# Packed attention, gated MLP and mixture of attentions: the last score groups behind the value products, the first query product behind the packed tokens' product, the softmax chain of the next item earlier

## The chip, the cores and the metric

One of the eight cores of a Trainium2 chip runs the whole kernel in one launch. The metric is the device time of that core in microseconds (us), the median of several runs. Engines are named as the profile names them: PE (TensorE, matmuls; PEld its weight loads), DVE (VectorE), ACT (ScalarE), POOL (GpSimd) and SP, whose queue issues the DMAs.

## What is computed

Eight batch items, 576 tokens each, go through three stages.

```python
# 1: attention of 32 packed tokens p over k and v, then of q over the packed result (8 heads of 64)
p_packed = sm_attn(p, k, v)
x = sm_attn(q, p_packed, p_packed)          # then heads side by side: 576 x 512
# 2: gated MLP with a product over the tokens
h = gelu(x @ w_in); u, v = h[..., :512], h[..., 512:]
v_s = einsum('ts,bsd->btd', w_sg, layer_norm(v) * g_ln) + b_sg
x = x + (u * v_s) @ w_out
# 3: four causal attentions of head size 64, each token takes the two with the largest logits x @ w_gate
for e in range(4):
    a = softmax(causal(scale * (x @ wq[e]) @ (x @ wk[e]).T))
    out += weight_of_e * (a @ (x @ wv[e]) @ wo[e])
```

All inputs and outputs are float32.

## The kernel before

The eight items form a software pipeline. While PE works on the third stage's attention of item b-1, it also does the second stage of item b and the first stage of item b+1. Products that need float32 accuracy are made of three passes over parts `hi` and `lo` in the type fp32r (`PASSES`); the part `hi` is an ACT copy, the part `lo` a subtraction on DVE or POOL (`lo_part`, L81).

PE's instructions stand in the order in which the Python code issues them (`manual_schedule` for PE). The instructions of ACT, DVE, POOL and SP are put in order by the framework's scheduler, from dependences and priorities, before the kernel runs. Every PE result goes to one of four PSUM tiles of two banks each (`pd`, `NPS = 4`); a product can only start when an earlier user of its tile has been read out by ACT or DVE. SBUF tiles come from pools in the same way: `NB["C"] = 4` tiles hold the split attention weights `a2h`, `a2l` of both head groups Q (two each), so the tiles of item b+1 are the ones that item b's last readers give back.

One item's work, with the names that the rows use:

- First stage (`p1_steps`): `natT`, `remT` transpose k and q on PE, `kT`, `qT` are their copies; `s1` makes the packed tokens' scores (tile `s`, L349) and their softmax (`a`), `a1T` transposes it, `pp` multiplies with v (L384), `ppT` transposes the result (L401); `s2` makes q's scores over the packed tokens (tile `s` again), DVE transposes them to `bt` (L411), POOL subtracts the maximum (L417), ACT exponentiates (L418), DVE divides and transposes back to `a2f` (L425). `split_a2` makes `a2h` on ACT (L465) and `a2l` on POOL.
- Second stage: `wp_mm`, `wp_out` fold the packed tokens into the input weights (`wp`, L474, parts `wph`, `wpl`); `v_tiles` are the value products (`v`, L519) with gelu and layer norm; `u_tile` (L556); `vs_tile` is the product over tokens (L570), whose gated result is `gh`, `gl`.
- `bdw` folds the packed tokens into the third stage's weights (`bdq`, `bdv`, L474: the packed tokens' product of this change's name). `qk(b, i)` for i from 0 to 3 makes queries and keys (L599, L604), `qk_mm` the product and `qk_out` its read-out. `vlog` makes the values and gate logits (L629, L633), `gates` the gates.
- Third stage: ten work items per batch item, numbered by (128-token row block j, pair of experts pr): number 2j+pr. `S0` to `S9` are the score groups (tile `sc`): PE product, maximum `nm` on DVE, two exponentials on ACT, normalisation on DVE (`at`). S8 and S9 (`att_last`, L707 and L713) take two PSUM tiles each. `T0` to `T9` transpose the weights (`aTp`, copies `aT` on ACT), `y0` to `y4` multiply with the values, one per row block, and `o0` to `o4` are the output products with their DMAs. `y`j needs T2j and T2j+1; the loop in `yv` does the first pair, then the second.

`front` issues the value products and `u_tile`s, `back` all the rest of an item; the strings given to `go` are the third stage's work of the item before. Between the attention strings, `run` mixes the list `main` with the first-stage steps of item b+1: at each turn the list with the smaller share of its summed cost done is served. The costs (4.0, 4.8, ...) set only this order.

Of the kernel before, what the change touches and what calls it, by code (L numbers as in the profile page):

```python
# [25 lines left out]
def packed_attention_mlp_moe_kernel(  # L26
# [39 lines left out]
    def slot(tag, dt=F32, w=None, name=None):  # L66
        t = sb.tile([P, BY[tag]], dt, tag=tag, name=name or ("s" + tag), bufs=NB[tag])
        return t if w is None else t[:, :w]
# [11 lines left out]
    def lo_part(eng, o, x, hi):  # L80
        eng.tensor_tensor(o, x, hi.bitcast(F32), op=OP.subtract)  # L81
# [375 lines left out]
    def split_a2(b, Q):  # L457
        s = ST[b]
        f = s.pop(("a2f", Q))
        hi, lo = slot("C", F32R, name="a2h"), slot("C", F32R, name="a2l")  # L460
        f = f.rearrange("p (a i) -> p i a", a=2)
        for o, i0, n in ((0, 0, S), (S, 256, 64)):
            src = f[:, i0:i0 + n // 2, :]
            dh, dl = (t[:, o:o + n].rearrange("p (i a) -> p i a", a=2) for t in (hi, lo))
            nc.scalar.activation(dh, src, AF.Copy)  # L465
            lo_part(nc.gpsimd, dl, src, dh)
        s["a2", Q] = (hi, lo)
# [44 lines left out]
    def v_tiles(b, cs):  # L512
        s = ST[b]
        pt2 = pd("v")
        for ci, c in enumerate(cs):
            n = 0
            for x, y in PASSES:
                for Q in range(2):
                    nc.tensor.matmul(pt2[:, ci, :], s["a2", Q][x][:, c * P:(c + 1) * P], wp_part(b, 1, y, Q),  # L519
                                     start=n == 0, stop=n == 5)  # L520
                    n += 1
        for ci, c in enumerate(cs):
            pt = pt2[:, ci, :]
            vg = slot("t", w=512, name="vg")
            nc.scalar.activation(vg, pt, AF.Gelu_apprx_tanh)
            st = small.tile([P, 6], F32, name="bnst")
            nc.vector.bn_stats(st, vg)
            mv = small.tile([P, 2], F32, name="mv")
            nc.vector.bn_aggr(mv, st)
            rstd = small.tile([P, 1], F32, name="rstd")  # L530
            nc.vector.tensor_scalar(rstd, mv[:, 1:2], LN_EPS, None, op0=OP.add)
            nc.gpsimd.tensor_tensor(rstd, rstd, mhalf, op=OP.pow)
            nc.vector.scalar_tensor_tensor(vg, vg, mv[:, 0:1], g_bc, op0=OP.subtract, op1=OP.mult)
            hi, lo = slot("B", F32R, 512, name="vnh"), slot("B", F32R, 512, name="vnl")
            nc.scalar.activation(hi, vg, AF.Copy, scale=rstd)
            if c < 4:
                nc.vector.scalar_tensor_tensor(lo, vg, rstd, hi.bitcast(F32), op0=OP.mult, op1=OP.subtract)
            else:
                nc.vector.scalar_tensor_tensor(hi[64:P], vg[64:P], rstd[64:P], hi[64:P].bitcast(F32),
                                               op0=OP.mult, op1=OP.subtract)  # L540
                nc.vector.memset(lo[64:P].bitcast(F32), 1.0)
                nc.scalar.activation(lo[:64], vg[:64], AF.Copy, scale=rstd[:64])
            s["vn", c] = (hi, lo)
# [4 lines left out]
    def u_tile(b, m):  # L548
        s = ST[b]
        u = slot("D", name="u")  # L550
        pt = pd("u")
        n = 0
        for x, y in PASSES:
            for Q in range(2):
                for h in range(2):
                    nc.tensor.matmul(pt[:, h, :HALF], wp_part(b, 0, y, Q)[:, m * P:(m + 1) * P],  # L556
                                     s["a2", Q][x][:, hs(h)], start=n == 0, stop=n == 5)
                n += 1
        nc.scalar.activation(two(u), pt[:, :, :HALF], AF.Gelu_apprx_tanh)
        s["u", m] = u  # L560
# [26 lines left out]
    def qk(b, i):  # L587
        qk_mm(b, i)
        qk_out(b, i)

    def qk_mm(b, i):

        s = ST[b]
        o = s["qkp", i] = pd("qk")[:, :, :HALF]
        cols = slice(i * P, (i + 1) * P)
        for m in range(4):
            for x, y in PASSES:
                for h in range(2):
                    nc.tensor.matmul(o[:, h, :], W["w_qk"][y][:, m, cols], s["g", m][x][:, hs(h)],  # L599
                                     start=(m, x, y) == (0, 0, 0), stop=False)  # L600
        for Q in range(2):
            for x, y in PASSES:
                for h in range(2):
                    nc.tensor.matmul(o[:, h, :], s["bd", Q][y][:, cols], s["a2", Q][x][:, hs(h)],  # L604
                                     start=False, stop=(Q, x, y) == (1, 1, 0))
# [199 lines left out]
    VT = ((0, 1), (2, 3), (4,))  # L805
# [24 lines left out]
    def front(b, go):  # L830

        v_tiles(b, VT[0])
        v_tiles(b, VT[1])
        v_tiles(b, VT[2])
        go("T0")
        for m in range(4):
            u_tile(b, m)

    def back(b, go, extra=()):
        main = []  # L840

        def add(cost, fn, *a):
            main.append((cost, lambda: fn(*a)))

        go("S1")
        vs_tile(b, 0)
        go("T1 S3 y0")
        vs_tile(b, 1)
        go("T2 S5 o0 T3")
        vs_tile(b, 2)  # L850
        go("y1 T4 S6")
        vs_tile(b, 3)
        go("T5 o1 S7")
        bdw(b)
        weights(b + 1, ("in1", "in0"))
        nxt = attention(b)
        add(4.0, go, "y2 T6 S8")
        add(4.8, qk, b, 0)
        add(3.5, go, "T7 o2 S9")
        add(4.8, qk, b, 2)  # L860
        add(3.0, go, "y3 T8")
        add(2.7, go, "o3 T9")
        add(2.0, go, "y4")
        add(4.2, vlog, b, VT[0])
        add(1.0, go, "o4")
        add(4.2, vlog, b, VT[1])
        add(2.1, vlog, b, VT[2])
        add(0.0, gates, b)
        p1 = P1.pop(b + 1, [])
        cut = len(p1) - 2  # L870
        run(main, p1[:cut])
        if b + 2 < B:
            ahead(b + 2)
        for Q, (_, f) in enumerate(p1[cut:]):
            f()
            split_a2(b + 1, Q)
        qk(b, 1)
        nxt("S0 S2")
        if b + 1 == B:
            qk(b, 3)  # L880
            return nxt
        wp_mm(b + 1, 1)
        qk_mm(b, 3)
        wp_out(b + 1, 1)
        qk_out(b, 3)
        wprime(b + 1, 0)
        weights(b + 1, ("qk", "vg"))
        nxt("S4")
        return nxt

    P1 = {}
# [41 lines left out]
    with tc.manual_schedule(engines={mybir.EngineType.PE}):  # L933
        ahead(1)
        go = back(0, attention(-1))
        for b in range(1, B):
            front(b, go)
            go = back(b, go)
        go("S4 S1 T0 S3 T1 y0 T2 S5 o0 T3 y1 T4 S6 o1 T5 S7 y2 T6 S8 o2 T7 S9 y3 T8 o3 T9 y4 o4")


# [29 lines left out]
```

## Time and profile before

| What | us |
|---|---|
| Median of 3 runs | 1007.45 (1006.8 to 1008.74) |
| The profiled execution, whole time | 1005.63 |
| Its span in the trace | 1003.9 |
| PE busy | 895.2 (89%) |
| DVE busy | 568.5 (57%) |
| ACT busy | 475.8 (47%) |
| POOL busy | 119.9 (12%) |
| DMA, queue of SP | 24.9% of 16 engines |

The first 110 us prepare weights; from there the trace repeats with a period of some 113 us per item, and the last 50 us have only the attention of the last item left. A bracket at the end of a timeline row is the idle time of that engine just before the row and the instruction whose end the profile puts it down to. The granted clock is a share of PE's full rate of 2.4 GHz: 1.00 is that level, 0.50 is 1.2 GHz.

### The profile page before, as it was taken

Reading aid. Unit: us, or ns where it says so; the run is one execution under the profiler, and the core shown is the slowest. Engines: PE = TensorE matmul, PEld = TensorE weight load, DVE = VectorE, ACT = ScalarE, POOL = GpSimd, SP = SyncE. Lnnn points to the kernel's source line nnn. Section 1 sums busy time; section 2 is a strip of 40 time slices with the busy share of each in tenths; the row PEclk is TensorE's granted clock in tenths of the full one; section 3 lists DMA queues with packets and bytes.
Section 4 is the critical chain, followed back from the end, with each engine's and each line's share of the span. In section 5 each row is a group of like instructions: output and inputs, shape, how many; then the busy total and the mean of one; then the engine's idle time right before and its main releaser. Section 6 shows DMA issues by size and latency. Waiting matters only on the chain.

```text
span 1003.9 us, 19707 instructions
## 1 busy us (share of the span) xinstructions
PE 895.2 (89%) x8009; PEld 747.2 (74%) x8009; DVE 568.5 (57%) x1354; ACT 475.8 (47%) x1087; POOL 119.9 (12%) x120
## 2 busy tenths in 40 slices
PE   3529899899998999899998999999989999899987
PEld 2205788697877888697877888787868788687965
DVE  3897433865367543865367543864377543865154
ACT  4423523465436452565436452655436452554245
POOL 0565010210012000210012000200012000200000
PEclk9758899999999999999999999999998999999989
DMA  8863133103230143103320132104320231100001
GB/s 234 201 205 131 43 114 119 65 11 124 94 95 22 46 143 92 64 12 124 101 88 22 55 137 90 64 12 142 98 93 2 77 107 40 64 11 23 17 11 37
DMA packets 60191, 81.07 MB, mean 81 GB/s; under 512 B 15107, under 2 KB 48387, under 8 KB 57029
## 3 DMA queue, kind: packets, MB, share of 16 engines
q1 hardware_dynamic: 60100, 79.81, 24.9%
q8 instruction: 63, 1.03, 0.4%
q14 instruction: 28, 0.22, 0.1%
HBM read 66.68 MB, written 13.12 MB: 79 GB/s over the span
## 4 chain that ended last, share of the span: by engine, by line
PE 54%; DVE 16%; ACT 7%; POOL 2%; issue 2%; POOLq 0%; ACTq 0%
PE vs L570 7%; PE o L774 6%; PE qk L599 5%; PE vlog L629 5%; PE v L519 5%; PE y L759 4%; PE aTp L731 3%; PE sc L684 3%; PE qk L604 3%; PE natT L326 3%; PE vlog L633 2%; DVE at L695 2%; ACT at L691 2%; PE sc L713 2%; DVE nm L687 2%
## 5 line engine op out<-in xcount | busy, mean ns | idle before, releaser
L599 PE MATMUL qk<-gh,w_qk 128*128 128x288 f32 x512 | 94.0, 306 | 2.1 <-DVE bdq L81 1.5
L691 ACT ACTIVATE at<-sc,nm 128x256 f32<-128x256 f32 (+3 forms) x128 | 66.1, 524 | 57.2 <-DVE nm L687 55.4
L570 PE MATMUL vs<-w_sg,vnh 128*128 128x288 f32 x512 | 91.7, 301 | 0.0
L599 PEld LDWEIGHTS qk<-gh,w_qk 128*128 128x128 f32 x512 | 76.5, 194 | 13.8 <-DVE nm L687 5.0
L78 ACT ACTIVATE aT<-aTp 128x512 f32<-128x512 f32 (+4 forms) x160 | 61.0, 436 | 52.5 <-PE aTp L731 47.3
L417 POOL TENSOR_TENSOR bt<-bt,mx 128x576 f32<-128x576 f32 x14 | 16.3, 1162 | 577.4 <-DVE gsm L662 531.6
L570 PEld LDWEIGHTS vs<-w_sg,vnh 128*128 128x128 f32 x512 | 74.5, 189 | 4.2 <-DVE yl L81 2.5
L629 PE MATMUL vlog<-w_vg,gh 128*128 128x260 f32 (+1 forms) x320 | 60.6, 287 | 0.0
L687 DVE TENSOR_REDUCE nm<-sc 128x2 f32<-128x256 f32 (+3 forms) x64 | 51.7, 819 | 12.3 <-PE sc L684 11.2
L759 PE MATMUL y<-aT,v 128*64 128x128 f32 (+2 forms) x960 | 58.1, 264 | 0.4 <-ACT aT L78 0.4
L695 DVE TENSOR_SCALAR at<-at,sm,gw 128x256 f32<-128x256 f32 (+3 forms) x128 | 55.9, 478 | 2.3
L599 PE MATMUL qk<-gl,w_qk 128*128 128x288 f32 x256 | 55.4, 298 | 0.0
L759 PEld LDWEIGHTS y<-aT,v 128*64 128x64 f32 (+1 forms) x960 | 46.9, 137 | 11.3 <-issue 5.4
L774 PE MATMUL o<-w_o,yh 128*128 128x512 f32 (+1 forms) x160 | 53.8, 418 | 1.4 <-ACT yh L762 1.4
L570 PE MATMUL vs<-w_sg,vnl 128*128 128x288 f32 x256 | 54.8, 295 | 0.0
L731 PE MATMUL aTp<-ident,at 128*128 128x128 f32 x320 | 47.9, 280 | 5.7 <-DVE at L695 5.7
L635 ACT ACTIVATE v<-vlog 128x512 f32<-128x512 f32 (+1 forms) x24 | 12.6, 524 | 83.4 <-PE vlog L633 83.4
L629 PEld LDWEIGHTS vlog<-w_vg,gh 128*128 128x128 f32 (+1 forms) x320 | 47.5, 178 | 2.2
L684 PE MATMUL sc<-qk 64*128 64x128 f32 (+3 forms) x384 | 47.6, 352 | 0.2 <-DVE qk L81 0.2
L731 PEld LDWEIGHTS aTp<-ident,at 128*128 128x128 f32 x320 | 37.5, 142 | 13.1 <-issue 7.0
L578 DVE TENSOR_TENSOR gt<-vs,u 128x576 f32<-128x576 f32 x32 | 24.1, 754 | 39.4 <-PE vs L575 39.4
L519 PE MATMUL v<-wph,a2h 128*128 128x512 f32 x80 | 32.2, 477 | 14.8 <-ACT a2h L465 14.8
(210 smaller groups left out, 2098.5 us busy)
## 6 DMA issues: line engine op xcount, KB each, us to landing
w_in<-kept_in SPq DMA_DIRECT2D x14, 1024.0 KB
k<-in_k_dram SPq DMA_DIRECT2D x32, 256.0 KB
v<-in_v_dram SPq DMA_DIRECT2D x32, 256.0 KB
q<-in_q_dram SPq DMA_DIRECT2D x32, 256.0 KB
w_qk<-kept_qk SPq DMA_DIRECT2D x8, 1024.0 KB
out_dram<-ot SPq DMA_DIRECT2D x32, 256.0 KB
w_vg<-kept_vg SPq DMA_DIRECT2D x8, 520.0 KB
raw_w_qk<-in_moe_w_in_dram SPq DMA_DIRECT2D x8, 256.0 KB
```

The costliest lines, as they stand in the source:

```text
L78: nc.scalar.activation(o, i, AF.Copy, scale=scale)
L519: nc.tensor.matmul(pt2[:, ci, :], s["a2", Q][x][:, c * P:(c + 1) * P], wp_part(b, 1, y, Q), start=n == 0, stop=n == 5)
L570: nc.tensor.matmul(pt[:, h, :HALF], s["vn", c][x][:, cols], w_sg[y][:, c, hs(h)], start=(c, x, y) == (0, 0, 0), stop=False)
L599: nc.tensor.matmul(o[:, h, :], W["w_qk"][y][:, m, cols], s["g", m][x][:, hs(h)], start=(m, x, y) == (0, 0, 0), stop=False)
L629: nc.tensor.matmul(pt[:n, ci, :260], s["g", m][x][:, c * P:c * P + n], W["w_vg"][y][:, m, :], start=(m, x, y) == (0, 0, 0), stop=False)
L684: nc.tensor.matmul(pt[:, e, :L], qs[x][r, j * P:L], ks[y][r, :L], start=False, stop=i == 2, skip_group_check=True)
L687: nc.vector.tensor_reduce(nm, pt[:, :, :L], axis=AX.X, op=OP.max, negate=True)
L691: nc.scalar.activation(ats[e][:, :L], pt[:, e, :L], AF.Exp, bias=nm[:, e:e + 1], accum_out=sm[:, e:e + 1])
L695: nc.vector.tensor_scalar(ats[e][:, :L], ats[e][:, :L], sm[:, e:e + 1], s["w"][:, j, 2 * pr + e:2 * pr + e + 1], op0=OP.mult, op1=OP.mult)
L731: nc.tensor.transpose(pt[:, e, c * P:c * P + P], ats[e][:, c * P:c * P + P], ident)
L759: nc.tensor.matmul(pt[64 * e:64 * e + 64, pr * w:pr * w + w], s["v2"][:m, c, col:col + D], s["aT", pr, e, j][c][:m, :], start=c == 0, stop ...
L774: nc.tensor.matmul(pt[:n, :], ys[x][:, pr * n:pr * n + n], W["w_o"][y][:, pr, :], start=i == 0, stop=i == 5)
```

## The change

The order of the strings and steps in `front` and `back` is rewritten; no instruction's shape and no pool changes.

- `front`: `u_tile(b, 0)` goes ahead of T0.
- `back`, around the products over tokens: S4 (the fifth of the ten score groups) moves from the end of `back`, ahead of the value products, to the third `vs_tile`; T1, y0, T4 and their neighbours move accordingly.
- `back`, after `bdw`: `qk_mm(b, 0)` stands directly behind it, and y2, S7, S8, the read-out of that product, T6 and S9 follow, before the mixed part begins.
- The mixed part holds o2, `qk(b, 2)`, T7, y3, T8, o3, T9, y4 and the first `vlog`. The last two `s2` steps are taken out of the mix as before, but now o4 and the second `vlog` stand between them, and the third `vlog` and `gates` behind them. Both steps and their `split_a2` are issued under `high_priority(offset=150)`, which moves them ahead in the scheduler's order on ACT, DVE and POOL.
- The last item's string begins with T0 and has S4 later.

```diff
         v_tiles(b, VT[2])
+        u_tile(b, 0)
         go("T0")
-        for m in range(4):
+        for m in range(1, 4):
             u_tile(b, m)
...
         go("S1")
         vs_tile(b, 0)
-        go("T1 S3 y0")
+        go("S3")
         vs_tile(b, 1)
-        go("T2 S5 o0 T3")
+        go("T1 y0 T2 S5")
         vs_tile(b, 2)
-        go("y1 T4 S6")
+        go("T3 o0 S4 y1")
         vs_tile(b, 3)
-        go("T5 o1 S7")
+        go("T5 S6 o1 T4")
         bdw(b)
...
-        add(4.0, go, "y2 T6 S8")
-        add(4.8, qk, b, 0)
-        add(3.5, go, "T7 o2 S9")
+        qk_mm(b, 0)
+        go("y2 S7 S8")
+        qk_out(b, 0)
+        go("T6 S9")
+        add(2.0, go, "o2")
         add(4.8, qk, b, 2)
-        add(3.0, go, "y3 T8")
-        add(2.7, go, "o3 T9")
-        add(2.0, go, "y4")
+        add(2.9, go, "T7 y3")
+        add(2.2, go, "T8 o3")
+        add(3.1, go, "T9 y4")
         add(4.2, vlog, b, VT[0])
-        add(1.0, go, "o4")
-        add(4.2, vlog, b, VT[1])
-        add(2.1, vlog, b, VT[2])
-        add(0.0, gates, b)
...
-        for Q, (_, f) in enumerate(p1[cut:]):
-            f()
-            split_a2(b + 1, Q)
+        for Q in range(2):
+            if p1:
+                with tc.high_priority(offset=150):
+                    p1[cut + Q][1]()
+                    split_a2(b + 1, Q)
+            if Q == 0:
+                go("o4")
+                vlog(b, VT[1])
+        vlog(b, VT[2])
+        gates(b)
         qk(b, 1)
...
         weights(b + 1, ("qk", "vg"))
-        nxt("S4")
         return nxt
...
-        go("S4 S1 T0 S3 T1 y0 T2 S5 o0 T3 y1 T4 S6 o1 T5 S7 y2 T6 S8 o2 T7 S9 y3 T8 o3 T9 y4 o4")
+        go("T0 S1 S3 T1 y0 T2 S5 o0 T3 S4 y1 T5 S6 o1 T4 S7 y2 T6 S8 o2 T7 S9 y3 T8 o3 T9 y4 o4")
```

PE's order of a middle item after `bdw`, before: y2, T6, S8, then the first transposes of the next item's k (`LDWEIGHTS` rows load the mask's weights).

```order
L474 MATMUL bdv<-w_vg,ppT 32x260 x8
L759 MATMUL y<-aT,v_4138 64x128 x12
L731 MATMUL aTp<-ident,at 128x128 x8
L707 LDWEIGHTS identb
L707 MATMUL sc<-causal,identb 128x64
L707 LDWEIGHTS identb
L707 MATMUL sc<-causal,identb 128x64
L713 MATMUL sc<-qk 64x288 x12
L315 MATMUL pT<-ident,pn 128x128 x2
```

The same place after: the first query product (its last row here is L604) is ahead of y2, and S7, S8, T6 and S9 follow on each other.

```order
L604 MATMUL qk<-a2l,bdq 128x288 x2
L759 MATMUL y<-aT,v_4182 64x128 x12
L680 LDWEIGHTS identb
L680 MATMUL sc<-causal,identb 128x128
L680 LDWEIGHTS identb
L680 MATMUL sc<-causal,identb 128x128
L684 MATMUL sc<-qk 128x512 x6
L707 LDWEIGHTS identb
L707 MATMUL sc<-causal,identb 128x64
L707 LDWEIGHTS identb
L707 MATMUL sc<-causal,identb 128x64
L713 MATMUL sc<-qk 64x288 x12
```

Three score groups now stand close together where one stood. PE's order in the mixed part, before: the second group of k transposes is followed by T7 and o2.

```order
L326 MATMUL natT<-ident,k 128x128 x8
L328 MATMUL remT<-ident,kr 128x128
L731 MATMUL aTp<-ident,at 128x128 x8
L774 MATMUL o<-w_o_948,yh 128x512
L774 MATMUL o<-w_o_949,yh 128x512
```

After: the packed tokens' scores `s` stand directly behind the transposes of their k, and y3 directly behind T7.

```order
L349 MATMUL s_5332<-kT,pT 32x288 x8
L326 MATMUL natT<-ident,k 128x128 x8
L328 MATMUL remT<-ident,kr 128x128
L349 MATMUL s_5371<-kT,pT 32x288 x8
L731 MATMUL aTp<-ident,at 128x128 x8
L759 MATMUL y<-aT,v_4182 64x128 x16
```

What stood between a read-out and its user there is gone. ACT's order at the same place, after: the second softmax's exponential (`a_5382`) stands between T7's two copies `aT`.

```order
L334 ACTIVATE kT<-natT 128x2x256 x2
L358 ACTIVATE a_5343,st_5341<-s_5332,st_5341 128x576
L78 ACTIVATE aT<-aTp 128x512
L358 ACTIVATE a_5382,st_5380<-s_5371,st_5380 128x576
L78 ACTIVATE aT<-aTp 128x512
```

PE's order at q's scores over the packed tokens (`s_4367`, `s_4396`), before: both stand together, and the second query product follows.

```order
L401 MATMUL ppT<-ident,pp_4220 128x128
L401 MATMUL ppT<-ident,pp_4297 128x128
L349 MATMUL s_4367<-qT,ppT 32x288 x8
L349 MATMUL s_4396<-qT,ppT 32x288 x8
L599 MATMUL qk<-gh,w_qk_748 128x288 x2
```

After: o4 and the second `vlog` follow the first of them (the rest of o4 and 32 rows of `vlog` stand before the second).

```order
L401 MATMUL ppT<-ident,pp_4179 128x128
L401 MATMUL ppT<-ident,pp_4248 128x128
L349 MATMUL s_4274<-qT,ppT 32x288 x8
L774 MATMUL o<-w_o_948,yh 64x512
L774 MATMUL o<-w_o_949,yh 64x512
```

The first chain to `a2f` starts an output product and a `vlog` earlier, measured from the second query product.

## Rows read from the trace of the kernel before

**Rows 1.** The page, part 1: busy us (share of the span) xinstructions.

```profile
PE 895.2 (89%) x8009; PEld 747.2 (74%) x8009; DVE 568.5 (57%) x1354; ACT 475.8 (47%) x1087; POOL 119.9 (12%) x120
```

**Rows 2.** Waits of PE, whole span: line, waited for, us in total, times, longest.

```profile
PE v L519 <- ACT a2h L465: 14.8, 6, 2.5
PE ppT L401 <- DVE pp L395: 8.7, 8, 4.1
PE sc L707 <- DVE yl L81: 8.6, 7, 1.2
...
PE sc L707 <- DVE bdq L81: 5.8, 7, 0.8
PE aTp L731 <- DVE at L695: 5.7, 8, 3.2
...
PE wp L474 <- DVE bt L411: 5.5, 6, 0.9
```

**Rows 3.** Timeline of PE: start, us, instruction; value products and T0, two items.

```profile
301.55 0.49 PE L519 MATMUL v<-wph,a2h 128*128 128x512 f32 x1
...
313.35 0.38 PE L731 MATMUL aTp<-ident,at 128*128 128x128 f32 x2
...
638.96 0.29 PE L680 MATMUL sc<-causal,identb 128*128 128x128 bf16 x2
...
639.90 0.86 PE L519 MATMUL v<-wph,a2h 128*128 128x512 f32 x2
...
641.91 0.50 PE L519 MATMUL v<-wph,a2l 128*128 128x512 f32 x1 [0.46 <-POOL a2l L81]
...
647.74 0.38 PE L731 MATMUL aTp<-ident,at 128*128 128x128 f32 x2
```

**Rows 4.** Timeline of ACT and POOL, the item at 640: parts of the weights.

```profile
637.00 0.99 ACT L465 ACTIVATE a2h<-a2f 128x576 fp32r<-128x576 f32 x2 [0.51 <-PE qk L604]
...
640.28 1.87 POOL L81 TENSOR_TENSOR a2l<-a2f,a2h 128x576 fp32r<-128x576 f32 x2 [0.51 <-ACT a2h L465]
```

**Rows 5.** Stretches: busy us of each engine, then granted clock, DMA share, GB/s.

```profile
306.00:308.00 2.00, 1.85 (x4) 1.49 (x5) 1.04 (x4) 1.98 (x5) 0.39 (x2) 0.50 0.00 0
...
354.00:356.00 2.00, 2.00 (x16) 1.58 (x13) 1.34 (x2) 0.21 (x2) 0.00 (x0) 0.50 0.45 188
...
660.00:662.00 2.00, 1.02 (x10) 0.82 (x10) 1.60 (x5) 0.54 (x4) 0.00 (x0) 1.00 0.00 0
...
241.00:242.00 1.00, 0.47 (x7) 0.35 (x8) 0.48 (x1) 1.00 (x3) 0.00 (x0) 1.00 0.99 418
```

**Rows 6.** Timeline, item at 350: S7's maximum, its first exponential; then S9's products.

```profile
347.34 1.22 DVE L687 TENSOR_REDUCE nm<-sc 128x2 f32<-128x1024 f32 x1
...
348.60 0.69 ACT L691 ACTIVATE at<-sc,nm 128x512 f32<-128x512 f32 x1 [1.68 <-DVE nm L687]
...
366.43 1.00 PE L713 MATMUL sc<-qk 64*64 64x288 f32 x12
```

**Rows 7.** Timeline, item at 360: the next item's k, its softmax, and y3.

```profile
363.87 1.04 PE L731 MATMUL aTp<-ident,at 128*128 128x128 f32 x8
363.97 1.08 ACT L334 ACTIVATE kT<-natT 128x512 f32<-128x512 f32 x2 [1.02 <-PE natT L326]
...
364.94 0.75 ACT L358 ACTIVATE a<-s,st 128x576 f32<-128x576 f32 x1
...
373.79 0.75 DVE L356 TENSOR_REDUCE st<-s 128x1 f32<-128x576 f32 x1
374.10 1.97 PE L759 MATMUL y<-aT,v 128*64 128x128 f32 x32
```

**Rows 8.** Timeline of PE, preparation: `s` directly behind the transposes of its k.

```profile
16.25 1.69 PE L349 MATMUL s<-kT,pT 64*32 64x288 f32 x16 [2.55 <-ACT kT L334]
```

**Rows 9.** Timeline of PE, last item: y0 directly behind T1.

```profile
969.89 0.86 PE L759 MATMUL y<-aT,v 128*64 128x128 f32 x4 [0.44 <-ACT aT L78]
```

**Rows 10.** Timeline of PE, first item: its first query product.

```profile
143.96 0.79 PE L599 MATMUL qk<-gh,w_qk 128*128 128x288 f32 x4 [1.50 <-DVE bdq L81]
```

More of the change, by code (lines that the diff above doesn't have):

```diff
@@ L834, in front, with back @@
         v_tiles(b, VT[2])
+        u_tile(b, 0)
         go("T0")
-        for m in range(4):
+        for m in range(1, 4):
             u_tile(b, m)
-    def back(b, go, extra=()):
+    def back(b, go):
         main = []
```

## The prediction

> **What bounds the kernel now.** I began with the page's busy times: PE is busy for 895.2 of 1003.9 us and no other engine for more than 57% [rows 1]. PE's own work sets the time, and the change leaves that work as it is: what can be won is PE's waiting, and time in which PE runs at the lower of its two clock levels. So the list of PE's waits came second. It names few places, each once per item: the value products behind `a2h` (14.8 us in six waits), `ppT` behind `pp` (8.7), S8's first products behind `yl` and `bdq` (8.6 and 5.8, seven each), T1 and its like behind `at` (5.7), and `wp` behind `bt` (5.5) [rows 2]. The third view is the timeline at those places, the fourth the granted clock there.
>
> The value products show that a wait costs more than its own length. From their first product to T0 they take 313.35 - 301.55 = 11.80 us in an ordinary item; in the item at 640, the one in which the exponential before `a2f` came early, 647.74 - 639.90 = 7.84 with a wait of 0.46 for `a2l` [rows 3]. The difference of 3.96 us is more than the mean wait of 14.8 / 6 = 2.47 [rows 2]; about 1.5 is left, and the clock shows where it goes: behind the wait PE runs at 0.50, the level of 1.2 GHz [rows 5]. The same fall shows behind S8's two waits (0.50 from 354 to 356), though not in every item: from 241 to 242 it is 1.00 [rows 5]; of seven such places I find it at six. Behind T1's single wait in the item at 660 it stays at 1.00 [rows 5], and that wait was 1.5 us long. So waits of some 2 us mostly bring a fall, and one of 1.5 us brought none.
>
> **The change part by part.** The working is against the profiled execution, 1005.63 us, which is 1.8 below the median of the runs.
>
> The value products. q's scores over the packed tokens now come earlier, the first by an output product and a `vlog`, the second by a `vlog`, and S4 no longer stands between them and the value products. Their softmax chain then ends before its last constraint, which stays: the four tiles of `a2h` and `a2l` are still being read by the last `qk`. In the item at 640 `a2h` began when that `qk` let it (bracket 0.51 <- PE qk), and POOL's `a2l` ended what PE waited for [rows 4]. That item is my model for all. Against it, S4 (639.90 - 638.96 = 0.94 us) no longer covers [rows 3], and POOL's idle of 0.51 before the second `a2l` goes [rows 4]: the wait is 0.46 + 0.94 - 0.51 = 0.89, which is 0.43 more than there. Six items gain 3.96, seven lose 0.43: 23.8 - 3.0 = **20.8 us off**. Bounds: 23.8, and 0 if the chain is as late as now.
>
> `wp` waits for `bt` in six items because both score tiles were made just before it; now a `vlog` and a whole `qk` stand between: **5.5 off** [rows 2]. T1 moves behind the second `vs_tile`, so of the 5.7 for `at` all but the last item's longest of 3.2 goes: **2.5 off**. In the last item S4 no longer delays S1's softmax on DVE and ACT, but S1 now waits for the keys' read-out; of the 3.2 I take **2 off**, between 0 and 3.2. `ppT` keeps its order and its 8.7.
>
> S8 and S9. S8's waits (8.6 + 5.8 = 14.4 us) and six falls of the clock (6 x 1.5 = 9) go, since the first query product now stands between `bdw` and y2 and gives ACT and DVE time to read out `bdq` and `bdv`. But S7, S8, T6 and S9 now follow on each other. S9's first tile is free when S7's exponentials end: 1.22 of maximum and two times 0.69 [rows 6], some 2.6 us after S7's products; its second when S8's first exponential (0.75, by the same form in [rows 7]) has followed, some 3.5 us. PE covers this with S8 (1.00 by S9's products [rows 6]) and T6 (1.04 by T7's transposes [rows 7]). That leaves 1.4, and 0.2 at the next products for the same queue: 1.6 us in seven items, 11.2. Bounds per item: 0, if ACT runs ahead of my count, and 14.4 / 7 = 2.06, as S8 has now. For the clock, 1.4 is nearest to the wait of 1.5 that brought no fall; I count falls in two items of seven, 3 us. Net 14.4 + 9 - 11.2 - 3 = **9.2 off**.
>
> The packed tokens' scores `s` of the second head group now stand directly behind the transposes of their k. Before, T7 stood there: it began at 363.87, and the copies `kT` ended at 363.97 + 1.08 = 365.05 [rows 7]. The scores need the first copy to start and the second for their second half: 1.1 us lost in seven items, **7.7 on**. Below: 0 needs copies at no time, so 0.5 is the least (one copy); above: the one place of the trace with this order, in the preparation, waits 2.55 [rows 8].
>
> y3 stands directly behind T7, and ACT makes the second softmax's exponential between T7's two copies. Maximum 0.75, exponential 0.75 and a read-out of its sum, copy 0.54 [rows 7], with DVE's small steps ahead of the maximum: some 2.9 us after the scores; T7 and the first half of y3 (1.04 + 1.97 / 2 [rows 7]) cover 2.0. That is 0.9 in six items, **5.4 on** (0 to 12, should y3 wait the whole chain). y4 behind T9 likewise, with four copies of q ahead on ACT: 0.3 in six items, **1.8 on**, from 0 to the price of the next row. y0 behind T1 is shown by the last item, where it stands so already: 0.44 [rows 9], seven times **3.1 on**.
>
> The first item's query product no longer waits 1.50 [rows 10], but there no attention stands between the loads of q and v and their users, and the loads start where they did; I set one against the other, **0** (between 1.5 off and 3 on). The score groups, output products and DMAs that only change places cost nothing more: PE's products are the same, ACT and DVE are idle for half and 43% of the span [rows 1], and the next weights' loads keep their place behind `bdw`; if that cover went, it would show as waits at the places above.
>
> Sum: 20.8 + 5.5 + 2.5 + 2 + 9.2 - 7.7 - 5.4 - 1.8 - 3.1 = 22.0 off. From 1005.63 this gives 983.6; the median stands 1.8 higher, 985.4, and I say **986**.
>
> **The rivals.** First: the new waits in the transposes are hidden, because ACT is free there, and the clock never falls: 7.7 + 5.4 + 1.8 + 3 less, **968**. For it speaks ACT's idle half; against it the copies' own length, which no idle engine shortens.
>
> Second: the waits have the length that I take, but each brings a fall of the clock. S9 in five more items and the transposes in seven: 12 x 1.5 = 18 on, **1004**. For it: two waits close together brought the fall at S8; against: the 1.5 us at 660 without one [rows 5].
>
> Third: the wait at the value products is one of buffers, not of order, and stays with its fall: 20.8 back, **1007**, no change. The mechanism is that `a2h` cannot be written before the last `qk` has read the old one, whatever comes earlier. The item at 640 speaks against it, where the same buffers left 0.46 [rows 3]. The Trainium skill, "Perfetto Trace Analysis", section Optimization Strategy, says that a gap repeating on the engine that should be saturated can mean too little SBUF or PSUM for the next tile; by that, moving the chain would change nothing here. The trace agrees for S8's waits, which are for PSUM tiles, and disagrees for the larger part of this one.
>
> Fourth, slower: the transposes' scores wait as long as in the preparation, 2.55 each time, and the clock falls behind them and behind S9 in every item. That is 7 x 1.45 + 18 = 28 on, **1014**. It decides the sign from 22 us of extra loss, 3.1 per item. Against it: the preparation's wait was shared with weight work on ACT and DVE, of which this part has none.
>
> That the change isn't in the program can be left at 2%: the orders of PE and ACT show it.
>
> **How the numbers follow.** The forecast has 0.52, the first rival 0.20, the second 0.10, the third 0.06, the fourth 0.10, an idle change 0.02. About 0.2% (2 us) is what a measurement of this kernel can tell from no change. Faster: 0.52 + 0.20 + 0.10 = 0.82; within 0.2%: 0.06 + 0.02 = 0.08; slower 0.10. The range takes in most of the first rival and, above, the second's edge: 969 to 1003.
>
> **What would show it.** Right: in the waits of PE, the value products wait about 0.9 for `a2l` and no longer for `a2h`; `wp` behind `bt` is gone; S9 takes S8's place with 1.4 in two waits; new rows name `s` behind `kT` (1.1 an item) and y3 behind `aT` (0.9). The granted clock is 1.00 from the second item to the last but for a few stretches, and the period of an item falls from some 113 us to some 110. Wrong: `a2h` still named with 2.5; waits at S9 or at the transposes above 2 us; or PE behind DVE at the products over tokens, since the layer norms must keep up with value products that end some 3 us earlier.

## The result, and the profile after

The changed kernel takes 980.5 us (median of four runs, 979.7 to 981.5) beside 1007.1 of the kernel before: a ratio of 0.974, interval 0.9725 to 0.9756. The forecast was 986 in a range from 969 to 1003. The profiled execution takes 980.57 us, with a span of 978.8, which is 25.1 less than before.

The page, part 1, of the changed kernel, and the granted clock of part 2, against [rows 1]:

```profile
PE 884.6 (90%) x8009; PEld 734.4 (75%) x8009; DVE 556.6 (57%) x1354; ACT 476.9 (49%) x1087; POOL 119.7 (12%) x120
...
PEclk9758899999999999999999999999999999999999
```

The same 8009 matmuls keep PE busy 10.6 us less, and the rest of the 25.1, 14.5 us, is idle time. The first figure is mostly the clock, less what the rows of `y` grew by (58.1 to 63.7 us; a wait inside a row counts as busy): from 200 to 900 us every stretch of 100 us has a granted clock of 1.00, where before it was 0.97 or 0.98 in most.

The waits of PE in the changed kernel (line, waited for, us in total, times, longest), against [rows 2]:

```profile
PE ppT L401 <- DVE pp L395: 8.7, 8, 4.1
...
PE v L519 <- POOL a2l L81: 6.8, 7, 1.0
...
PE y L759 <- ACT aT L78: 6.6, 13, 0.9
...
PE sc L707 <- ACT at L691: 4.8, 7, 0.7
PE s L349 <- DVE kT L335: 4.5, 7, 0.6
PE sc L707 <- ACT at L719: 3.7, 7, 0.5
...
PE qk L599 <- ACT at L719: 2.2, 6, 0.4
...
PE aTp L731 <- DVE at L695: 1.5, 1, 1.5
```

The rows for `a2h`, for `yl` and `bdq` at S8 and for `bt` are gone; `a2l`, S9 (two `sc` rows and one `qk` row), `s` and y3 have taken their place. The timeline of PE shows where the largest gain is, against [rows 3] (start, us, instruction, and in brackets the idle time before it):

```profile
408.23 0.72 PE L519 MATMUL v<-wph,a2h 128*128 128x512 f32 x2
...
410.62 0.50 PE L519 MATMUL v<-wph,a2l 128*128 128x512 f32 x1 [0.96 <-POOL a2l L81]
...
416.41 0.69 PE L556 MATMUL u<-a2h,wph 128*128 128x288 f32 x4
```

The value products take 416.41 - 408.23 = 8.18 us where they took 11.80.

The starts of three of PE's rows, the first `bdq`, the first `v` and the first `u` of each item, cut both traces into stretches; together the stretches are the whole difference:

| Stretch, us | before | after | all of them |
|---|---|---|---|
| start to the first `bdq` | 139.57 | 139.93 | +0.4 |
| first `bdq` to `v` | 50.49 | 49.36 | -1.1 |
| `bdq` to `v`, six items | 66.28 to 67.31 | 67.34 to 67.38 | +2.2 |
| `v` to `u`, seven items | 11.43 to 12.63, one 7.97 | 8.18 to 8.22 | -22.6 |
| `u` to the next `bdq`, seven | 33.74 to 33.78, one 35.56 | 33.89 to 33.90 | -0.9 |
| last `bdq` to the last product | 89.55 | 86.45 | -3.1 |

So the value products bring nearly all, and the part behind `bdw`, on which most of the prediction's terms rest, changes by 2 us. (S4, S7 and T0 go from one stretch to another, so the small differences are not the price of one move.)

### The profile page after: what moved, and what is told of

It reads as the page before. It is cut to its first block, busy times and chain, and to the rows that moved or that the text cites. A ratio compares the mean times of both kernels' runs of the same rounds, so it can differ in the third digit from the quotient of the medians.

```text
span 978.8 us, 19667 instructions
## 1 busy us (share of the span) xinstructions
PE 884.6 (90%) x8009; PEld 734.4 (75%) x8009; DVE 556.6 (57%) x1354; ACT 476.9 (49%) x1087; POOL 119.7 (12%) x120
## 4 chain that ended last, share of the span: by engine, by line
PE 77%; ACT 8%; DVE 7%; DMA 3%; issue 2%; POOL 2%; SPq 1%; ACTq 0%; DVEq 0%; POOLq 0%
PE vs L570 11%; PE qk L599 11%; PE vlog L629 6%; PE u L556 5%; PE v L519 5%; PE o L774 5%; PE y L759 5%; PE qk L604 4%; PE sc L684 4%; PE aTp L731 3%; PE vlog L633 3%; PE fold L257 2%; PE s L349 2%; ACT at L719 1%; PE natT L326 1%
## 5 line engine op out<-in xcount | busy, mean ns | idle before, releaser
L599 PE MATMUL qk<-gh,w_qk 128*128 128x288 f32 x512 | 91.3, 300 | 2.2 <-ACT at L719 2.2
L691 ACT ACTIVATE at<-sc,nm 128x256 f32<-128x256 f32 (+3 forms) x128 | 66.3, 525 | 53.4 <-DVE nm L687 53.2
L599 PEld LDWEIGHTS qk<-gh,w_qk 128*128 128x128 f32 x512 | 74.5, 188 | 13.1 <-DVE nm L687 5.0
L759 PE MATMUL y<-aT,v 128*64 128x128 f32 (+2 forms) x960 | 63.7, 264 | 6.6 <-ACT aT L78 6.6
L759 PEld LDWEIGHTS y<-aT,v 128*64 128x64 f32 (+1 forms) x960 | 49.0, 136 | 20.2 <-ACT aT L78 11.6
L687 DVE TENSOR_REDUCE nm<-sc 128x2 f32<-128x256 f32 (+2 forms) x64 | 52.0, 821 | 12.0 <-PE sc L684 11.5
L695 DVE TENSOR_SCALAR at<-at,sm,gw 128x256 f32<-128x256 f32 (+3 forms) x128 | 51.3, 443 | 2.0
L629 PE MATMUL vlog<-w_vg,gl 128*128 128x260 f32 (+1 forms) x160 | 45.1, 282 | 0.0
L604 PE MATMUL qk<-a2h,bdq 128*128 128x288 f32 x256 | 44.3, 295 | 0.0
```

Of the source, the lines that this page charges most:

```text
L629: nc.tensor.matmul(pt[:n, ci, :260], s["g", m][x][:, c * P:c * P + n], W["w_vg"][y][:, m, :], start=(m, x, y) == (0, 0, 0), stop=False)
L687: nc.vector.tensor_reduce(nm, pt[:, :, :L], axis=AX.X, op=OP.max, negate=True)
L691: nc.scalar.activation(ats[e][:, :L], pt[:, e, :L], AF.Exp, bias=nm[:, e:e + 1], accum_out=sm[:, e:e + 1])
L695: nc.vector.tensor_scalar(ats[e][:, :L], ats[e][:, :L], sm[:, e:e + 1], s["w"][:, j, 2 * pr + e:2 * pr + e + 1], op0=OP.mult, op1=OP.mult)
L759: nc.tensor.matmul(pt[64 * e:64 * e + 64, pr * w:pr * w + w], s["v2"][:m, c, col:col + D], s["aT", pr, e, j][c][:m, :], start=c == 0, stop ...
```

## The experiments

The theory: the second softmax chain of `a2f` ended too late, and this cost the wait and the clock; the rest of the change moves waits from one place to another. The rivals: the buffers hold `a2h` back; the part behind `bdw` carries the gain.

**The chain put back.** The changed kernel, with both `s2` steps again together behind all `vlog`, and without their priority.

```diff
-        for Q in range(2):
-            if p1:
-                with tc.high_priority(offset=150):
-                    p1[cut + Q][1]()
-                    split_a2(b + 1, Q)
-            if Q == 0:
-                go("o4")
-                vlog(b, VT[1])
-        vlog(b, VT[2])
-        gates(b)
+        for Q, (_, f) in enumerate(p1[cut:]):
+            f()
+            split_a2(b + 1, Q)
```

(o4, the other `vlog` and `gates` go back into the mix.)

> The changed kernel with one part undone: the two score steps of the softmax chain stand together again behind all of vlog, without priority. My theory (the earlier chain is what ends the long wait at the value products): the wait for a2h is back, about 3.4 us an item since S4 no longer stands ahead, wp waits 0.9 for bt again, and the clock falls at the value products in most items: 7 x 4.3 less the 0.96 of now, and 6 or 7 falls of 1.5 us: some 1010 to 1016 us, slower than the kernel before. Rival (the wait is one of buffers, whatever comes earlier): no more than 0.5 us an item, 980 to 984 us.

Measured 1014.5 us, ratio 1.0085 (1.0061 to 1.0108). Its waits of PE:

```profile
PE v L519 <- ACT a2h L465: 23.8, 7, 3.4
...
PE wp L474 <- DVE bt L411: 6.5, 7, 0.9
```

The wait is back in all seven items, 0.9 longer than before because S4 no longer stands ahead of it, and `v` to `u` takes 12.3 to 13.5 us. The pools are those of the changed kernel, so what the buffers allow didn't change: order made this wait. The Trainium skill, "Perfetto Trace Analysis", section Optimization Strategy, says that a gap that repeats on the engine that should be saturated can mean missing room for the next tile; for this gap it did not, by two runs 34 us apart with the same tiles.

**The chain alone.** The kernel before, with only this part of the change.

```diff
-        for Q, (_, f) in enumerate(p1[cut:]):
-            f()
-            split_a2(b + 1, Q)
+        for Q in range(2):
+            if p1:
+                with tc.high_priority(offset=150):
+                    p1[cut + Q][1]()
+                    split_a2(b + 1, Q)
+            if Q == 0:
+                go("o4")
+                vlog(b, VT[1])
+        vlog(b, VT[2])
+        gates(b)
```

> The kernel before with one part alone: the softmax chain of the next item earlier, under priority. My theory: the value products then behave in all items as in the item at 640 of the kernel before (wait 0.5 for a2l, no fall of the clock), wp's wait for bt goes, T1 waits 1.5 us: 6 x 2.3 + 5.5 us off, 986 to 990 us, with the falls of the clock behind S8 left. Rival (it needs the other parts): 1000 us or more.

Measured 983.5 us, ratio 0.978 (0.975 to 0.981): 23 to 24 of the 26.6 us, and less than the 986 to 990 expected. Its waits of PE:

```profile
PE aTp L731 <- DVE at L695: 13.5, 8, 2.9
...
PE sc L707 <- DVE yl L81: 8.6, 7, 1.2
...
PE sc L707 <- DVE bdq L81: 5.8, 7, 0.8
```

S8's waits are as before, the value products wait for nothing, and T1's wait for its weights has grown from 5.7 us to 13.5: part of what the value products no longer lose is lost there. Behind T1's 1.5 us the clock falls in four of the seven items (`u` to `bdq` takes 36.6 to 36.7 us in these, 35.1 in the other three).

What the edit does to the second chain shows in both traces: PE's last score product, then DVE's first and last step to `a2f`. Before, in the item whose `v` starts at 414.23:

```profile
397.80 1.20 PE L349 MATMUL s<-qT,ppT 64*32 64x288 f32 x32
...
405.32 0.80 DVE L411 STREAM_TRANSPOSE bt<-s 128x288 f32<-128x288 f32 x2
...
415.52 0.77 DVE L425 STREAM_TRANSPOSE a2f<-bt 128x576 f32<-128x576 f32 x1
```

In the changed kernel, in the item whose `v` starts at 298.76:

```profile
282.68 0.72 PE L349 MATMUL s<-qT,ppT 64*32 64x288 f32 x16
...
283.59 0.83 DVE L411 STREAM_TRANSPOSE bt<-s 128x288 f32<-128x288 f32 x2
...
289.71 0.78 DVE L425 STREAM_TRANSPOSE a2f<-bt 128x576 f32<-128x576 f32 x1
```

The second scores end 15.2 us ahead of `v` before and 15.4 after, so they come no earlier. What shrank is the chain behind them, from 17.3 us to 7.1: before, DVE started it only 6.3 us after the scores, directly behind the first chain, and later did steps of the attention and of the weights between its own. The edit moves the first chain ahead and gives both priority. No run has one without the other, so it is not shown which of the two shortened the chain.

**The part behind `bdw` undone**, in the changed kernel:

```diff
-        go("T5 S6 o1 T4")
+        go("T5 S6 o1 T4 S7")
...
-        qk_mm(b, 0)
-        go("y2 S7 S8")
-        qk_out(b, 0)
-        go("T6 S9")
+        add(4.0, go, "y2 T6 S8")
+        add(4.8, qk, b, 0)
+        add(3.5, go, "T7 o2 S9")
...
```

> The changed kernel with the part behind bdw undone: the first query product goes back into the mixed part, S7 ahead of bdw, and y2, T6, S8, T7, o2, S9 mix as before. My theory: S8's two waits of 2.06 us and the falls of the clock behind them are back (7 x 2.06 + 6 x 1.5 = 23 us on), S9's waits of 1.57 and the waits of the packed tokens' scores (1.08), y3 (0.66) and y4 (0.28) go (11 + 7.6 + 4 + 1.7 = 24 us off): about 980 us, no change, since this part only trades. Rival (the first query product behind bdw is the main gain): 990 us or more. In either case the granted clock should fall in most items near S8.

Measured 981.3 us, ratio 0.975 (0.972 to 0.977): not to be told from the changed kernel. Its waits of PE:

```profile
PE sc L707 <- DVE bdq L81: 6.6, 7, 1.0
...
PE u L556 <- ACT vg L525: 6.1, 6, 1.0
...
PE aTp L731 <- ACT at L691: 4.8, 7, 0.7
```

The clock falls at four of seven places behind `bdw` here, in the changed kernel at none; it comes to the same time. But the two times differ by more than this part. From `u` to the next `bdq` this kernel takes 36.2 us instead of 33.9 in six items. S7, which here stands in that stretch, makes 1.1 of the 2.3; the other 1.2 go with the new wait at `u`, which is that of a late table load, as the runs further down show. Without it this kernel would take some 974 us (an estimate, six times 1.2 less; not run). By this estimate the part alone is a loss of some 6 us, and the trade comes out even only through the load.

**The front part undone**, in the changed kernel: S4 ahead of the value products again, T1 and y0 behind the first `vs_tile`, T0 ahead of all `u_tile`s.

```diff
-        go("S3")
+        go("T1 S3 y0")
         vs_tile(b, 1)
-        go("T1 y0 T2 S5")
+        go("T2 S5 o0 T3")
...
+        nxt("S4")
```

> The changed kernel with the part ahead of bdw undone: S4 stands ahead of the value products again, T1 directly behind the first product over tokens, T0 ahead of all u tiles. My theory: the value products wait about 0.5 instead of 0.96 because S4 covers it, S4's exponentials delay the layer norms on ACT, and T1 waits 1.5 us for its softmax as it did in the item at 660: about 7 us on, 985 to 989 us, the clock at its full level in all items. Rival (this part is idle): 978 to 982 us.

Measured 989.0 us, ratio 0.9825 (0.9802 to 0.9848): 8.5 us for the front part. T1's wait is 12.1 us longer (13.6 us in eight, 1.5 in the changed kernel). That is more than S4's cover of `a2l` gives, which is back here (`v` to `u` 7.4 instead of 8.2). And the clock, expected at its full level in all items, falls behind T1 in two of seven (`u` to `bdq` 35.6 us there, 34.1 in the others).

**The value products pass by pass.** In the changed kernel the wait for POOL's `a2l` is the largest of the new ones. Eight products instead of four now stand ahead of its first reader:

```diff
-        for ci, c in enumerate(cs):
-            n = 0
-            for x, y in PASSES:
+        for n, (x, y) in enumerate(PASSES):
+            for ci, c in enumerate(cs):
...
-                                     start=n == 0, stop=n == 5)
-                    n += 1
+                                     start=n == 0 and Q == 0, stop=n == 2 and Q == 1)
```

> The changed kernel, but the value products run pass by pass over both token tiles instead of tile by tile, so the first product that reads a2l comes after eight products instead of four. Nothing is left out. In the changed kernel PE waits 0.96 us for POOL's a2l, seven times (6.8). Theory (this wait is POOL's work on the second a2l, so four more products of 0.24 us ahead of it cover it): the wait falls below 0.1, 6 to 7 us off, 973 to 976, and the second head group's a2l takes no wait either. Rival (the wait only moves: to the second a2l, or to DVE behind the products, whose layer norms then get both tiles late instead of one after the other): 979 to 983.

Measured 973.3 us, ratio 0.967 (0.9653 to 0.9687), 7.2 off the changed kernel. No row for `v` is left among the waits, and `v` to `u` takes 7.3. Whether more tiles for `a2h` and `a2l` would do the same was not tried.

**S9's wait doubled**, to see what the clock does:

```diff
-        go("T6 S9")
+        go("S9 T6")
```

> The changed kernel with T6 behind S9 instead of ahead of it. Nothing is left out. T6's transposes (1.04 us) no longer cover S9's wait for its PSUM tile, so that wait grows from 1.2 to about 2.2 us in seven items. This asks what the clock does behind it. Theory (waits of some 2 us bring a fall, as behind S8 in the kernel before; waits of 1.6 us bring none): 7 x 1.0 for the wait and 7 x 1.5 for falls, 17 to 18 on: 996 to 999. Rival (the clock stays at 1.00, the falls of the kernel before had another cause): 7 on, 987 to 989. Second rival (T6 stands elsewhere but S9's tile was not what ended the wait): 980 to 982.

Measured 989.2 us, ratio 0.983 (0.981 to 0.985), 8.7 over the changed kernel: between the two, just above the rival's. S9's own wait grew to 1.57, not 2.2; where the clock held, the next users of PSUM tiles waited too, in the item at 575 for 0.66 us at `pT` and 0.54 at `natT`. PE's timeline at two of the seven places:

```profile
464.38 0.19 PE L707 MATMUL sc<-causal,identb 128*128 128x64 bf16 x1 [1.57 <-ACT at L691]
464.50 1.70 PE L713 MATMUL sc<-qk 64*64 64x288 f32 x12
...
575.03 0.19 PE L707 MATMUL sc<-causal,identb 128*128 128x64 bf16 x1 [1.57 <-ACT at L691]
575.15 1.00 PE L713 MATMUL sc<-qk 64*64 64x288 f32 x12
...
579.24 0.44 PE L315 MATMUL pT<-ident,pn 128*128 128x128 f32 x2 [0.66 <-ACT at L719]
```

And the stretches there, and one behind the second waits of the item at 352 (busy us of each engine, then the granted clock):

```profile
464.00:466.00 2.00, 1.61 (x13) 1.19 (x12) 1.56 (x6) 1.96 (x6) 0.00 (x0) 0.62 0.00 0
...
575.00:577.00 2.00, 1.97 (x22) 1.63 (x21) 1.66 (x7) 1.63 (x4) 0.00 (x0) 1.00 0.00 0
359.00:361.00 2.00, 2.00 (x11) 2.00 (x10) 0.00 (x0) 0.69 (x2) 0.00 (x0) 0.50 0.75 252
```

The same wait, to a hundredth of a microsecond, brought a fall at 464 and none at 575; of the seven items three had one right behind it and one, the item at 352, behind the two waits that follow. And a fall has no fixed price. At 464 the slower products (1.70 instead of 1.00) use up the time in which PE would have waited at `pT`: `bdq` to `v` takes 68.58 us there. In the three items with a fall right behind the wait this stretch takes 68.30, 68.58 and 68.89, in the two whole items without one 68.28 and 68.90: no difference shows. Where the fall came later, over the query product at 358, the same stretch takes 70.43, 1.5 more than in the item at 575, which has the same waits.

**The part behind `bdw` by hand.** Between each read-out and its user stands another product; the steps of the next item no longer go by costs.

```diff
-        go("T6 S9")
-        add(2.0, go, "o2")
-        add(4.8, qk, b, 2)
-        add(2.9, go, "T7 y3")
...
+        go("T6 o2 S9")
+        p(2 + 2)
+        qk(b, 2)
+        p(1 + 1 + 2)
+        go("T7")
+        p(1)
+        p(1 + 2)
+        go("y3")
...
+            ppT0()
+            pp1()
```

(`p(n)` issues the next n first-stage steps.)

> The changed kernel with the part behind the packed tokens' product put in an order by hand: o2 goes between T6 and S9; q's transposes or k's stand between each copy and its user (the third query product ahead of the scores s, T7 ahead of the second s, a qT group ahead of y3 and y4, pp ahead of ppT). Nothing is left out. In the changed kernel these places wait 1.57 (S9), 1.08 (s), 0.66 (y3), 0.28 (y4) and 1.2 (ppT) us an item. Theory (each of these waits is a read-out that directly precedes its user, and any other product between them covers it): 3 to 4 of the 4.8 us an item go, seven items, 21 to 28 off: 953 to 960. Rival (ACT and DVE are the bound of this part, so the waits only move to the next users of PSUM tiles): 975 to 984.

Measured 965.5 us, ratio 0.959 (0.958 to 0.961), 15.0 off where 21 to 28 were expected. Where it was meant, it gave what it should: `bdq` to `v` falls from 67.35 to 64.0, 3.35 in six items and about 1 in the first, some 21 us. But from `u` to the next `bdq` each item but the first takes 1.3 longer. PE and ACT at the second `u_tile` of this kernel:

```profile
512.47 1.28 ACT L525 ACT_TABLE_LOAD   x1 [3.00 <-issue]
513.77 1.09 ACT L525 ACTIVATE vg<-v 128x512 f32<-128x512 f32 x2
...
519.30 0.79 PE L556 MATMUL u<-a2h,wph 128*128 128x288 f32 x4 [1.01 <-ACT vg L525]
```

And ACT in the changed kernel:

```profile
409.58 1.28 ACT L525 ACT_TABLE_LOAD   x1
412.53 1.09 ACT L525 ACTIVATE vg<-v 128x512 f32<-128x512 f32 x2 [1.67 <-PE v L519]
```

ACT's instructions stand in the same order in both. In the changed kernel the function table is loaded ahead of the products' end, here behind it, and the gelus that free the `u_tile`'s PSUM tile are late by it. The traces show what holds the load: here ACT's wait for the first value products, a semaphore instruction of L525, stands ahead of the load and lasts 4.12 us, to 512.44; in the changed kernel the gelu itself has that wait, behind the load. The kernel with the part undone, above, has the same row for `u`, and so has the one with the chain put back (5.0 us in six).

**Both edits.**

> Both edits together: the value products pass by pass, and the part behind the packed tokens' product in the order by hand. Nothing is left out. If the two are independent the gains add: 947 to 954. If either only moves its wait, it gives what the other gives alone.

Measured 958.0 us, ratio 0.952 (0.9503 to 0.9536): 22.5 off the changed kernel, 7.2 + 15.0 to 0.3 us. The 947 to 954 expected were missed because the order by hand gave less than expected. The waits that stood at S9 have only moved on to whoever asks for a PSUM tile next, o2 behind S7's exponentials and the third query product behind S9's:

```profile
452.31 0.73 PE L772 MATMUL o<-w_o,yh 128*128 128x512 f32 x2 [0.68 <-ACT at L689]
...
457.47 0.79 PE L597 MATMUL qk<-gh,w_qk 128*128 128x288 f32 x4 [0.83 <-ACT at L717]
```

**The score groups pulled apart.** There are four PSUM tiles, and a score group holds its own until its exponentials end. So the wait falls on the fourth tile behind it.

```diff
+        go("S7")
         qk_mm(b, 0)
-        go("y2 S7 S8")
+        go("y2 T6")
         qk_out(b, 0)
-        go("T6 o2 S9")
-        p(2 + 2)
+        go("S8 o2")
         qk(b, 2)
-        p(1 + 1 + 2)
-        go("T7")
+        p(2 + 2)
+        go("T7 S9")
...
```

> The kernel with both edits (value products pass by pass, part behind the packed tokens' product by hand), with S7, S8 and S9 pulled apart: S7 stands ahead of the first query product, S8 behind T6, S9 behind the third query product and T7, and the first-stage steps of the next item stand so that each PSUM tile is asked for again only after more than 3.5 us of other products. Nothing is left out. The kernel with both edits still waits 0.68 us at o2 for S7's exponentials and 0.83 at the third query product for S9's, 1.5 us in seven items. Theory (each score group keeps its PSUM tiles for 2.6 to 3.5 us after its products, and the wait falls on whoever asks for a tile fourth behind it, so that distance and not order as such decides): both waits go, 9 to 11 us off the 958.0, 947 to 949. Rival (ACT, on which the exponentials and all copies queue, is the bound of this part): the waits only move to s, y3 or the output products, 955 to 960.

Measured 945.6 us, ratio 0.940 (0.938 to 0.942), 12.3 off where 9 to 11 were expected. Its waits of PE:

```profile
PE u L554 <- ACT vg L523: 5.8, 6, 1.0
...
PE s L349 <- DVE kT L335: 2.4, 7, 0.6
```

Nothing of S7 to S9 is left; `bdq` to `v` takes 61.8 us. Other distances were not tried.

**The table loaded early.**

```diff
+        junk = small.tile([P, 1], F32, name="junk", bufs=1)
+        nc.scalar.activation(junk, ST[b + 1]["wp", 0][0][:, :1].bitcast(F32), AF.Gelu_apprx_tanh)
         weights(b + 1, ("qk", "vg"))
```

> The kernel with the score groups pulled apart, plus one gelu of a single column on ACT, read from the first-stage weights wph and used by nobody, directly ahead of the value products' own gelus. Nothing is left out. That kernel, and every one whose part behind the packed tokens' product was not as in the changed kernel, waits 1.0 us at the second u_tile for ACT's gelu (5.8 in six items); there the load of ACT's function table (1.28 us) starts only after the first value products, idle 2.1 to 3.0 us before it, while in the changed kernel the same load starts directly behind the copy wph. Theory (the late table load is what makes the gelus late): with the table loaded early the wait goes, 5 to 6 us off 945.6, 939 to 941. Rival (the gelus queue behind the layer norm's copies vnh, whatever the table does): 945 to 947.

Measured 938.0 us, ratio 0.931 (0.930 to 0.933), 7.6 off where 5 to 6 were expected. ACT in this kernel:

```profile
394.05 1.01 ACT L485 ACTIVATE wph<-wp 128x1024 fp32r<-128x1024 f32 x1
395.08 1.28 ACT L917 ACT_TABLE_LOAD   x1
396.38 0.20 ACT L917 ACTIVATE junk<-wph 128x1 f32<-128x1 f32 x1
397.14 1.09 ACT L523 ACTIVATE vg<-v 128x512 f32<-128x512 f32 x2 [0.56 <-PE v L518]
```

The row for `u` behind `vg` is gone, `u` to `bdq` takes 33.9 us instead of 35.1, and ACT's other instructions stand in the same order as without the edit: it was the load, not the queue of copies. The expectation goes too far with "every one": the kernel with the chain put back has the wait, with the part behind `bdw` as in the changed kernel, and the chain alone has the old part and no such wait. This is the fastest version, 42.5 us under the changed kernel.

## Why the prediction was right

The sign, the place and most terms held; the reason given for the largest held only in part.

- **Value products**: 20.8 forecast. By the stretches `v` to `u`, with T0's 0.14 taken off where it stood in between, 21.6. The wait for `a2l` is 0.96 (0.89 forecast), and in the item at 640 the stretch grew by 0.35 as the sum had it (0.43). The chain alone and the chain put back show that the chain is the cause. But the forecast had both chains start earlier, and the second, which ends last, does not (its scores end 15.4 us ahead of `v` beside 15.2): it is 10.2 us shorter. The priority, part of the edit that did this, has no place in the forecast's reasons.
- **`wp` behind `bt`**, 5.5: gone, and back with the chain put back. **T1**: of 5.7 the last item's 1.5 is left, 4.2 off beside 2.5 + 2; the wait comes back with S4's old place.
- **S8 and S9**, 9.2 forecast. Mis-sized twice, with the errors nearly cancelling. The falls behind S8 were put at 1.5 each, the price at the value products. But `bdq` to `v` of the kernel before takes 66.28 in the one item without a fall and 67.00 to 67.31 in the five with one: 0.7 to 1.0. Two other kernels agree (65.1 to 65.2 with a fall and 64.3 without, the part undone; 66.3 to 66.4 and 65.4, the chain alone). So some 6 x 0.85 = 5.1 us were to be won there and not 9. On the other side the falls assumed behind S9, two of seven for 3 us, did not come. That makes 14.4 + 5.1 - 10.7 = 8.8. S9's wait is as counted, in the timeline of PE in the changed kernel, with the other new waits behind it:

```profile
352.72 0.19 PE L707 MATMUL sc<-causal,identb 128*128 128x64 bf16 x1 [0.68 <-ACT at L691]
353.44 0.19 PE L707 MATMUL sc<-causal,identb 128*128 128x64 bf16 x1 [0.53 <-ACT at L719]
...
357.83 0.79 PE L599 MATMUL qk<-gh,w_qk 128*128 128x288 f32 x4 [0.37 <-ACT at L719]
...
365.28 1.13 PE L349 MATMUL s<-kT,pT 64*32 64x288 f32 x16 [0.64 <-DVE kT L335]
...
369.33 1.09 PE L759 MATMUL y<-aT,v 128*64 128x128 f32 x14 [0.66 <-ACT aT L78]
...
376.61 0.95 PE L759 MATMUL y<-aT,v 128*64 128x64 f32 x20 [0.28 <-ACT aT L78]
...
432.46 1.04 PE L759 MATMUL y<-aT,v 128*64 128x128 f32 x8
```

  0.68 + 0.53 + 0.37 = 1.58, where 1.6 was forecast; of it 0.37 stands at the next query product, where I had 0.2.
- **`s` behind `kT`**, 7.7: the bracket says 0.64, and the row is 1.13 long where it was 0.71 before (the second half waits inside it): 1.06 in seven items, 7.4. **y3**: 0.66 in six items, 4.0 for 5.4. **y4**: 0.28, 1.7 for 1.8. **y0**: no bracket, but its row of eight products takes 1.04 where it took 0.66 before: 0.38 in seven, 2.7 for 3.1. The two rows before:

```profile
362.19 0.71 PE L349 MATMUL s<-kT,pT 64*32 64x288 f32 x16
...
325.90 0.66 PE L759 MATMUL y<-aT,v 128*64 128x128 f32 x8
```

- **First and last item**: the first query product waits no more (1.5 off), the first item's transposes wait 0.75 more (`natT` 0.44, `a1T` 0.30); in the last item y0 waits 0.9 instead of 0.44 [rows 9]. Together 0.3 off, where I had 0 besides T1.

Together: 21.6 + 5.5 + 4.2 + 8.8 - 7.4 - 4.0 - 1.7 - 2.7 + 0.3 = 24.6 of the 25.1 us; 0.5 stays unassigned. The forecast's 22.0 was low by 3.1, of which y3 makes 1.4, the value products 0.8. The other 2.4 us between 986 and 980.5 are the 1.8 added for the distance of the profiled execution from the median, which the changed kernel does not have, and rounding.

Of the rivals, the hidden waits (968) fell: the copies' length shows at every place named. The falls at every new wait (1004) fell in this kernel, though with S9 ahead of T6 they came in four of seven items; the 1.5 us at 660 without a fall, on which the forecast leaned, was thus a case and no bound, as T1's waits of the same length show too, with a fall in four of seven items of the chain alone. That none came at S9 here is luck in part. The buffer wait (1007) fell with the chain put back. The fourth, slower (1014), fell too: the scores `s` wait 1.06 and not 2.55, without a fall.

What the prediction did not draw from its own sum is that the part behind `bdw` loses by itself: a gain of 9.2 against a loss of 14.9 in the transposes, 5.7 on, with 5.5 from `bt` on the chain's account. With its terms as measured this is 8.8 against 13.1, 4.3 on. Undone, the time stays within the intervals, but with the late table load in it; less that load the part costs some 6 us by the estimate above, of the size that the sum says.

## What to carry to other kernels

Cut both traces at the same few instructions and compare the stretches item by item: that shows at once which of several moves pays, and the price of a clock fall from items that differ in nothing else. In a ring of few PSUM tiles, put behind a long read-out (a maximum and exponentials) as much PE work as it lasts before the ring comes round, since a shorter cover only hands the wait to the next user. Before a part that was undone is called worth nothing, look in that run's list of waits for one that the undoing brought in. When a wait names an activation, look at the row ahead of it for a table load that starts late.

## What the runs showed of the hardware

- Waits of equal length (1.57 us) were followed at once by a granted clock at the lower level of 1.2 GHz in three items, and not in four; T1's waits of 1.5 us in four of seven items of the chain alone and in two of seven with the front part undone. A fall cost about 1.5 us at the value products and behind T1 and 0.7 to 1.0 behind S8; with S9 ahead of T6, where PE would have waited a little later anyway, nothing that shows (68.30 to 68.89 us with it, 68.28 and 68.90 without).
- ACT's load of a function table, 1.28 us, is placed by where its wait stands: it started directly behind the last copy, or 2.1 to 5.0 us later where ACT's wait for the value products stood ahead of it. One early gelu of a single column took 7.6 us off a kernel of 946. The Trainium skill, "ScalarE: Activation LUTs", section What ACT_TABLE_LOAD costs, gives 1283 ns for the load, with which the row agrees, and a further 1380 ns of draining; here the next ACT row starts 0.02 us behind the load, so that part does not show.
